# TensorE's head as loops, with the first instruction a jump to the last block of code, in a one-core decode kernel

## The chip, the cores and the metric

The kernel runs on one core of one Trainium2 chip. The metric is the device time of one execution in microseconds (us), lower is better. Before the change it was 1292.78 us (median of 3 runs, 1292.63 to 1292.84). A single profile is one execution, and its own time is quoted where that matters.

Names used below: TensorE (PE) multiplies matrices, VectorE (DVE) and ScalarE (ACT) do element-wise work, GpSimd (POOL) sets up constants, SyncE (SP) issues the large loads. A large load is spread over 16 data engines (each has 16 completions in the trace). "Products" are VectorE's multiplications of keys by the query; the first of them begins the main loop.

## The reference, cut to what matters

```python
B, Sq, D = 8, 1, 576          # A: attention over a cache
H, Sk, Dh = 32, 4096, 128     # k_cache, v_cache: (8, 32, 4096, 128) bf16, 268 MB each
F = 4608                      # B: a feed-forward layer

def reference(A_x, A_k_cache, A_v_cache, A_wq, A_wo, B_x, B_w1, B_b1, B_w2, B_b2):
    xn = layernorm(A_x)
    q = (xn @ A_wq) as heads
    p = softmax(q k^T * Dh ** -0.5)
    attention = (p v) as rows @ A_wo
    y = layernorm(xn)
    mlp = gelu(y @ B_w1 + B_b1) @ B_w2 + B_b2
    return A_x + attention + mlp
```

The two caches have to be read once: 537 MB of the 557 MB that the kernel moves.

## The kernel before

It has three stages. The **head** computes the queries, broadcasts them over the partitions, and computes the hidden layer of the feed-forward part while the first tiles of the caches arrive. The **main loop** goes through 32 pairs of a key tile and a value tile. The **tail** multiplies by `B_w2` and `A_wo`, which are loaded last.

All large loads go through SyncE's queue in order. The buffer `ring` is one block short of three tiles, and at first the head's weights lie in it too, so the loads of the main loop wait for room:

```python
    od.load("sync", "wq", ring[:, 0:WQ_END], wq_v)      # load "w q"
    od.load("sync", "w1", ring[:, W1_AT:RING], w1_v)
    load_kv(k_v, 0, 0)                                  # first key tile, "k0"
    ...
    for token in (wq_read, *head_done):                 # queries and broadcasts done
        od.wait("sync", token)
    load_kv(v_v, 0, 1)                                  # "v0", over wq
    for token in mlp_done:                              # hidden layer done
        od.wait("sync", token)
    for t in range(1, NT):
        sy.wait_ge(sem["kf"], NX * (t - 1) + 2)         # two blocks of tile t-1 multiplied
        load_kv(k_v, t, 0)                              # "k1", over w1 and the head's rooms
        sy.wait_ge(sem["vf"], t)
        load_kv(v_v, t, 1)                              # "v1"
    ...
    for n, (r0, r1) in enumerate(zip(CUTS, CUTS[1:])):  # A_wo in four pieces
        sy.dma_start(out=wo_rows(r0, r1), in_=wo_v[:, r0 * D:r1 * D]).then_inc(wo_in[-1], 16)
```

TensorE's part of the head is unrolled. The queries are 36 matmuls with 32 columns of weights each, four of which use the four column groups of the array at once (in the trace four start within 0.04 us, and the next four 0.43 us later). The broadcasts are eight times four matmuls, of which two use half the array each (two start within 0.01 us), and ScalarE copies every result out:

```python
    def queries(e):
        for c in range(WC):                             # WC = 9
            wv = wq_sb[:, c, :].rearrange("p (x m d) -> p m x d", m=M, d=Dh)
            for m in range(M):                          # M = 4, the column groups
                i = e.matmul(
                    S_ps[0][m * MP:(m + 1) * MP, :], lhsT=xT[:, c, :], rhs=wv[:, m],
                    start=(c == 0), stop=(c == WC - 1))
        return i
    ...
    for b in range(B):
        ps, key = (tot_ps, "tot") if b % 2 else (oT_ps, "oT")
        ...
        pe(["q", "sel"], [key], broadcast)              # 4 matmuls, two abreast
        act([key], [f"qb{b}"], lambda e: e.activation(out=dst, in_=t, func=ACT.Copy))
    ...
    te.br("head")                                       # TensorE's code is in blocks of its own
```

In the tail, TensorE waits for `B_w2`, then for each piece of `A_wo`. Behind the third piece are 18 matmuls, then the result is copied and stored.

The softmax here doesn't subtract the row's maximum and nothing guards it: scores larger than these inputs give would overflow.

## Time and profile before

| what | before | where it is read |
|---|---|---|
| span of the profiled run | 1291.5 us | head of the page |
| load queue's share of 16 engines' span | 99.7% | queue table |
| PE, DVE busy | 57%, 64% | table of engines |
| first product | 46.82 us | timeline of DVE |
| k1 issued | 53.53 us | timeline of SP |
| k1's data would be missed from about | 62 us | v0 has landed on its first engine at 63.49; an issue takes about 1.5 us to become data |
| third piece of A_wo landed | 1286.88 (13 engines), 1288.26 us (the last) | trace, semaphore updates of that load |

The queue table of the page comes first. Its columns are packets, MB, and the time of those packets as a share of 16 engines' span.

```profile
q1 hardware_dynamic: 10368, 556.93, 99.7%
q8 instruction: 3, 0.05, 0.0%
q10 hardware_dynamic: 38, 0.02, 0.0%
q14 instruction: 1, 0.01, 0.0%
```

The load queue leaves nothing free, so the kernel is bound by the loads, and nothing that an engine does faster can help unless it changes how the data engines are used. Four packets of *instructions* are in the table too. Their share is 0.0%, but this is the mean of 16 engines. That each of them sits on one engine, and on one that the loads use, is read from the landings below: after each of the first three, one more engine of the loads is late.

The chain of waits that ended last, in order of time (start us, us, what), ends on a load:

```profile
1259.74 28.52 DMA ring<-in_A_wo_dram
1288.26 0.04 issue
1288.31 1.29 PE acc L374 x18
1289.60 0.02 issue
1289.62 0.45 DVE fin L604
```

1288.26 is when the *last* of 16 data engines delivered its part of the third piece of A_wo; thirteen of them had delivered at 1286.88. The following table, worked out from the single packets of the trace, shows where that comes from. For a load, the spread is how much later than the first engine each of the last engines finished:

```text
kernel before        first engine, us   spread of the last three engines, us
w q                       12.6            0.50  0.51  0.75
k0                        44.2            0.51  0.75  1.75    (one engine late)
v0                        63.5            0.50  1.68  1.78    (two)
k1                        82.8            1.69  1.80  1.91    (three)
main loop from here on                    1.72  1.82  1.94    (three, to the end)

packets of instructions: queue 8 at 29.9, 76.0 and 1287.1 us (16,384 bytes, 1.02 to 1.09 us each),
                         queue 14 at 52.1 us (8,192 bytes)
```

Each fetch leaves one more engine about 1.2 us later than it was (the last values step from about 0.5 to about 1.7), and late to the end of the run: the queue is 99.7% busy.

The timeline of SP shows when loads are issued (columns: start us, us, engine line operation, out<-in):

```profile
0.00 0.38 SPq L96 DMA_DIRECT2D ring<-in_A_wq_dram  x1
...
1.26 0.33 SPq L271 DMA_DIRECT2D ring<-in_A_k_cache_dram  x1
23.95 0.33 SPq L271 DMA_DIRECT2D ring<-in_A_v_cache_dram  x1
53.53 0.33 SPq L271 DMA_DIRECT2D ring<-in_A_k_cache_dram  x1
74.24 0.33 SPq L271 DMA_DIRECT2D ring<-in_A_v_cache_dram  x1
```

Each tile takes 19.33 us of all engines. k1, issued at 53.53, had 63.49 as its deadline; v1, issued at 74.24, had 82.82.

The timelines of PE, ACT and DVE in the head (in brackets, the idle time before and what ended it):

```profile
13.84 4.01 PE L367 MATMUL s_ps<-ring 128*32 128x512 bf16 x36 [1.36 <-DVE quad L354]
18.55 0.41 PE L394 MATMUL oT_ps<-ring 128*64 128x256 bf16 x4 [0.36 <-ACT ring L385]
20.10 0.60 ACT L402 ACTIVATE qb<-oT_ps 128x512 bf16<-128x512 f32 x1
20.60 0.59 ACT L402 ACTIVATE qb<-tot_ps 128x512 bf16<-128x512 f32 x1
26.02 0.85 PE L414 MATMUL o_ps<-ring 128*32 128x384 bf16 x3 [2.80 <-DMA ring<-in_B_w_dram]
46.82 6.70 DVE L559 TENSOR_TENSOR ring<-ring,qb 128x4096 bf16<-128x4096 bf16 x3 [0.32 <-DVE hT_sb L445]
```

The queries took 4.01 us. Four broadcast matmuls took 0.41 us, less than the 0.60 us of the copy behind them, and the copies follow each other with at most 0.13 us between them: the broadcasts ran at ScalarE's pace. The layer then waited 2.80 us for `B_w1`.

### The profile page before, as it was taken

To read this page: it belongs to the slowest core of one execution; us is meant where nothing else is said; L and a number is where in the kernel's file an instruction comes from. 1 tells how busy PE (TensorE), PEld (TensorE's weight loads), DVE (VectorE), ACT (ScalarE), POOL (GpSimd) and SP (SyncE) were. 2 spreads that over 40 slices of the span, in tenths; PEclk is the share of its full clock that TensorE was granted. 3 is DMA by queue.
4 is the path that set the end of the run, shared out by engine and by line. 5 is a ranking of instruction groups with operands and counts; after the bars stand their busy time and mean duration, and the time that the engine had idled before them with its cause. 6 is when DMAs were issued, how large, how long until landed. Compare 5 with 4: busy or idle time off the path is not lost. (4 is left out here: it accounts for less than half of the span.)

```text
span 1291.5 us, 14658 instructions
## 1 busy us (share of the span) xinstructions
PE 736.8 (57%) x4707; PEld 322.3 (25%) x4707; DVE 829.4 (64%) x740; ACT 56.8 (4%) x181; POOL 2.4 (0%) x12
## 2 busy tenths in 40 slices
PE   4654565554565554665554565554566554565557
PEld 1222232222222222222222232222222222222223
DVE  2655677655677655677655677655677655577654
ACT  2000000000000000000000000000000000000000
POOL 0000000000000000000000000000000000000000
PEclk8778887778887777887777887778887777888779
DMA  9999999999999999999999999999999999999998
GB/s 419 441 427 440 430 428 449 422 428 449 422 428 449 422 430 447 422 436 440 424 436 438 426 438 434 428 442 428 428 449 422 428 449 422 428 449 422 430 447 350
DMA packets 10410, 557.02 MB, mean 431 GB/s; under 512 B 1163, under 2 KB 1188, under 8 KB 1446
## 3 DMA queue, kind: packets, MB, share of 16 engines
q1 hardware_dynamic: 10368, 556.93, 99.7%
q8 instruction: 3, 0.05, 0.0%
q10 hardware_dynamic: 38, 0.02, 0.0%
q14 instruction: 1, 0.01, 0.0%
HBM read 556.94 MB, written 0.01 MB: 431 GB/s over the span
## 5 line engine op out<-in xcount | busy, mean ns | idle before, releaser
L643 PE MATMUL s_ps<-ring,ident 128*128 x2048 | 544.5, 423 | 514.1 <-PEq L641 513.1
L559 DVE TENSOR_TENSOR ring<-ring,qb 128x4096 bf16<-128x4096 bf16 x256 | 579.2, 2283 | 281.6 <-DMA ring<-in_A_k_cache_dram 281.3
L643 PEld LDWEIGHTS s_ps<-ring,ident 128*128 128x128 bf16 x2048 | 217.4, 106 | 828.3 <-issue 678.5
L534 DVE TENSOR_REDUCE sc<-s_ps 128x32 f32<-128x512 f32 x256 | 171.8, 684 | 0.0
L662 PE MATMUL o_ps<-ring,ebd 128*32 128x512 bf16 x2048 | 116.4, 380 | 0.0
L546 DVE TENSOR_TENSOR ebd<-es,head 128x1536 bf16<-128x1536 bf16 x64 | 77.9, 1218 | 0.0
L569 DVE RECIPROCAL rec<-tot_ps 128x8 f32<-128x8 f32 x32 | 6.6, 208 | 110.7 <-PE oT_ps L670 110.7
L582 ACT ACTIVATE es<-sc 128x192 bf16<-128x192 f32 x64 | 19.8, 310 | 1104.2 <-DVE sc L534 1104.2
L662 PEld LDWEIGHTS o_ps<-ring,ebd 128*32 128x32 bf16 x2048 | 51.6, 97 | 62.5 <-issue 13.6
L670 PE MATMUL oT_ps<-selc,ob 128*128 128x8 f32 x256 | 33.9, 259 | 12.3 <-ACT ob L586 12.3
L670 PEld LDWEIGHTS oT_ps<-selc,ob 128*128 128x128 f32 x256 | 31.0, 191 | 15.2 <-ACT ob L586 15.2
L586 ACT ACTIVATE ob<-o_ps 128x512 f32<-128x512 f32 x32 | 19.1, 597 | 80.2 <-PE o_ps L662 80.2
L425 DVE TENSOR_SCALAR ring<-ring 96x384 f32<-96x384 f32 x2 | 0.7, 352 | 26.4 <-ACT ring L424 26.4
L545 DVE TENSOR_TENSOR Es<-Ep 128x1 f32<-128x1 f32 x32 | 5.1, 160 | 13.3 <-ACT es L582 13.3
L666 PEld LDWEIGHTS tot_ps<-headf,Es 128*128 128x128 f32 x64 | 9.5, 187 | 13.6 <-issue 13.6
L666 PE MATMUL tot_ps<-headf,Es 128*128 128x8 f32 x64 | 12.4, 266 | 0.0
L582 ACT ACTIVATION_READ_ACCUMULATOR es<-sc 128x1 f32 x64 | 11.9, 186 | 0.0
L414 PE MATMUL o_ps<-ring 128*32 128x384 bf16 x27 | 7.8, 860 | 2.8 <-DMA ring<-in_B_w_dram 2.8
L574 DVE TENSOR_TENSOR Ox<-on,quad 128x32 bf16 x32 | 6.2, 192 | 4.8
L414 PE MATMUL s_ps<-ring 128*32 128x384 bf16 x27 | 7.9, 862 | 0.0
L374 PE MATMUL acc<-ring,hT_sb 128*8 128x288 bf16 x72 | 6.0, 335 | 2.8 <-DMA ring<-in_B_w_dram 2.8
L336 PE MATMUL tot_ps<-ident,ring 40*128 40x16 bf16 x9 | 0.7, 204 | 11.8 <-DVE ring L314 11.8
(76 smaller groups left out, 61.2 us busy)
## 6 DMA issues: line engine op xcount, KB each, us to landing
ring<-in_B_w_dram SPq DMA_DIRECT2D x2, 5184.0 KB, 25.2
ring<-in_A_wq_dram SPq DMA_DIRECT2D x1, 4608.0 KB, 13.7
ring<-in_A_wo_dram SPq DMA_DIRECT2D x1, 1728.0 KB, 28.6
ring<-in_A_wo_dram SPq DMA_DIRECT2D x1, 1584.0 KB, 26.5
ring<-in_A_wo_dram SPq DMA_DIRECT2D x1, 1008.0 KB, 28.5
ring<-in_A_k_cache_dram SPq DMA_DIRECT2D x32, 31.9
ring<-in_A_v_cache_dram SPq DMA_DIRECT2D x32, 30.5
ring<-in_A_wo_dram SPq DMA_DIRECT2D x1, 288.0 KB, 28.8
```

The lines of the kernel that those rows point to most:

```text
L414: i = e.matmul(h_ps[j][s * MP:(s + 1) * MP], lhsT=lhsT, rhs=wv[:, r0:r0 + HK, :], **flags)
L534: ins = ve.tensor_reduce(out=sc[:, n * CB:(n + 1) * CB], in_=bank_of(x).rearrange("p (c d) -> p c d", d=DL), axis=AX.X, op=ALU.add)
L546: ve.tensor_tensor(out=ebd[:, ja:jb], in0=es[:, a:b].rearrange("p (j c) -> p j c", c=4).unsqueeze(2) .to_broadcast([P, nj, G, 4]), in1=hea ...
L559: ve.tensor_tensor(out=k, in0=k, in1=qb[:, bass.ds(t, 1), :].to_broadcast([P, CB, Dh]), op=ALU.mult,).then_inc(sem["prod"], 1)
L569: ve.reciprocal(out=rec[:], in_=tot_ps[:, :G]).then_inc(sem["rec"], 1)
L574: ve.tensor_tensor(out=Ox[:, bass.ds(t, 1)].rearrange("p o g m -> p (o g) m"), in0=on[:].unsqueeze(2).to_broadcast([P, G, M]), in1=quad[:] ...
L582: sa.activation(out=es[:, a * CB:b * CB], in_=sc[:, a * CB:b * CB], func=ACT.Exp, scale=scale, accum_out=Ep[:, i:i + 1]).then_inc(sem["x"], 1)
L586: sa.activation(out=ob[:].rearrange("r c d -> r (c d)"), in_=o_ps, func=ACT.Copy).then_inc(sem["ob"], 1)
L643: ins = te.matmul(to, lhsT=idn, rhs=k[:, :, d * DL:(d + 1) * DL], start=(d == 0), stop=(d == Dh // DL - 1))
L662: ins = te.matmul(o_ps[m * MP:(m + 1) * MP, :], lhsT=ebd[:, j].rearrange("p g c -> p (g c)"), rhs=vals[:, c:c + 4, :], start=(j < M), stop ...
L666: te.matmul(tot_ps[:, :G], lhsT=Es[:].to_broadcast([P, P]), rhs=headf[:], start=True, stop=True).then_inc(sem["vf"], 1)
L670: ins = te.matmul(oT_ps[:, :G], lhsT=ob[:, c, :], rhs=selc[:, c, :], start=(c == 0), stop=(c == 3))
```

## The change

Its intent: TensorE's program is fetched while data flows, and every fetch makes one data engine late. The author's idea was that a shorter program should need fewer fetches; that if the first instruction jumps to the last block of code, this block should be fetched before the queues are full; and that hints on the last branches should keep TensorE and VectorE from fetching beyond their ends. To shorten the program, queries and broadcasts become loops. A loop's matmul takes the places of its operands from registers. In the loops as written all of these start at partition 0, so that four matmuls abreast become four full-width ones in a row, with zeros in the weights where other column groups are. The layer goes in five groups (four of 512 columns and one of 256) in place of six of 384.

```diff
     def queries(e):
-        for c in range(WC):
-            wv = wq_sb[:, c, :].rearrange("p (x m d) -> p m x d", m=M, d=Dh)
+        def part(at, w, start):
+            wv = ring[:, bass.ds(w, HQ)].rearrange("p (x m d) -> p m x d", m=M, d=Dh)
             for m in range(M):
-                i = e.matmul(
-                    S_ps[0][m * MP:(m + 1) * MP, :], lhsT=xT[:, c, :], rhs=wv[:, m],
-                    start=(c == 0), stop=(c == WC - 1))
-        return i
+                e.matmul(
+                    S_ps[0], lhsT=xTz[:, bass.ds(at + (M - 1 - m) * MP, P)], rhs=wv[:, m],
+                    start=start and m == 0, stop=False)
+        part(0, 0, True)
+        (at, w), close = looped("queries", WC - 1, at=(M * MP, M * MP), w=(HQ, HQ))
+        part(at, w, False)
+        close()
+        return nothing(e, S_ps[0][:, :1], idn, xTz)
...
+    def broadcasts(e):
+        to = nc.alloc_registers("broadcast_to", engines=[ENG.PE])
+        nc.regs_mov(to, 0)
+        (at,), close = looped("broadcast", B, at=(0, MQ))
...
+        e.wait_ge(sem["free"], 1).then_inc(sem["free"], -1)
+        for v in range(2):
+            for k in reversed(range(NG)):
+                i = e.matmul(
+                    t[:(k + 1) * MQ, v * NH2:(v + 1) * NH2, :],
+                    lhsT=selz[:, bass.ds(at + (v * B + 1 - k) * MQ, (k + 1) * MQ)], rhs=q_v[:, k],
+                    start=True, stop=True)
+        i.then_inc(sem["full"], 1)
+        nc.regs_alu(to, NB, to, op=ALU.subtract)
+        close()
...
-    te.br("head")
+    te.br("tour")
...
+    ve.br("vector_end").branch_hint(vector_last)
+    block("vector_end", ENG.DVE)
...
+    te.br("tensor_end").branch_hint(tensor_last)
+    block("tour")
+    later(main.bb, nc.cur_bb.bb, ENG.PE)     # moves TensorE's drain and start barrier here
+    te.br("head")
+    block("tensor_end")
```

`later` moves TensorE's drain and its wait at the common start barrier behind the jump. So the other engines wait at the barrier until TensorE has jumped.

## The prediction

> **What bounds the kernel now.** DMA, end to end: the queue table gives 556.93 MB on the load queue at 99.7% of 16 engines' span; PE is busy 57%, DVE 64%. Every data engine carries 1/16 and never idles, so time lost on *one* engine is never made up: it shows where the last load waits for its slowest sixteenth. The chain of waits that ended last says this: A_wo load 28.5 us, PE acc 1.29, DVE fin 0.45, then the output store.
>
> **What the trace's packets show.** Four packets of instructions lie in the span: queue 8 (16,384 bytes, I read it as TensorE's) at 29.9, 76.0 and 1287.1 us, taking 1.02 to 1.09 us, and queue 14 (8,192 bytes; VectorE, I think) at 52.1 us. The first load's 16 completions spread over 0.75 us. After each of the first three fetches one more engine is late by about 1.2 us: the spread becomes 1.75 us by 44 us, and two, then three engines sit at +1.7 to +1.95 us from 83 us to the end. The last A_wo chunks land accordingly: 13 engines by 1287.62 us, the three late ones at 1288.77 to 1288.96; PE's last wait ends on them. [...]
>
> **The change.** Looping removes 116 TensorE instructions (791 to 675)[...]. The first jump makes TensorE fetch the last block before bulk data flows, and the hints should keep both engines from fetching past their ends. Intended: no fetch while the queues are full, so no late engine. Worth: 1288.96 - about 1287.7 = **1.2 us at the tail, all on the critical path**, if all three go. Removing only one or two gains about 0.1 us, since the remaining late engine still sets the end.
>
> **What it costs.** Queries become 36 full-width 512-column matmuls in sequence instead of four abreast: 4.0 us now; then about 9 cold at 0.427 us and 27 warm at 0.22 = about 10 us (estimate). Broadcasts stay bound by eight 0.6 us ACT copies. The layer begins when the copies end (about 30.5) instead of on w1 (26.0); five groups instead of six, the same columns, about 13 us as before; GELU chain about 6.5. Tile 0 starts at about 51 instead of 46.8. Slack: the second k load was issued at 53.5 with data queued to 63.5; the second v load at 74.2 with data to 82.8. Four microseconds later still leaves about 2 us after issue latency: no bubble, cost 0. TensorE reaching the start barrier a few us late delays only the k load (24 us of data queued ahead) and set-up work with slack.
>
> **Predicted:** 1291.7 us, 8 in 10 within 1291.1 to 1292.9. Faster by over 2%: 0.5%; within 2%: 98.5%; slower: 1%.
>
> **Right if:** queue 8 and VectorE's queue have no packets between about 5 us and the tail; the 16 completions of mid-run loads stay within about 0.8 us; the last A_wo landing is about 1.2 us earlier; first DVE product at 49 to 53 us; DMA share unchanged or nearer 100% with no gap at 60 to 90 us.
>
> **Wrong if:** the jump's fetch itself falls into the first data packets and leaves one engine 1.2 us late (no gain); a next-block fetch still comes when TensorE reaches its last block near 1280 us; VectorE's fetch stays; or the looped queries or broadcasts stall (branches, semaphores) over 6 us longer than now, and the second v load is issued after 81 us, when DMA runs dry and the kernel is 1 to 3 us slower.

The forecast's sum: 1292.8 us before, less 1.2 at the tail, plus nothing for the head, is about 1291.6, put at 1291.7. That 116 fewer instructions, with the jump and the hints, would take away all the fetches after the start was the author's estimate. In the estimate of the queries, 0.427 us is the spacing of the nine steps of the queries in the trace of the kernel before, and 0.22 that of its 512-column matmuls near 70 us; that nine would be slow was an estimate too (13 were).

## The result, and the profile after

The kernel after the change took 1296.62 us (median of 6 runs, 1296.29 to 1297.52), the kernel before 1292.94 us (6 runs of the same rounds). The ratio is 1.003, with a 95% interval from 1.0017 to 1.0043: slower by 0.3%, 3.7 us, which is inside the class "within 2%". A ratio here and below is the mean time of one kernel's fast runs over that of the other's of the same rounds, so it is not quite the ratio of the medians quoted. The six times lie in two groups, 1296.3 to 1296.8 and 1297.4 to 1297.5; the profiled run (1297.42 us, span 1296.1) is of the second.

The queue table after the change:

```profile
q1 hardware_dynamic: 10368, 556.93, 99.4%
q8 instruction: 1, 0.02, 0.0%
```

The fetches are gone, as intended: one is left, at 4.68 us, and queue 14 has none in the span. But the share of the load queue *fell*, from 99.7 to 99.4% of a longer span. The bytes are the same in both, so about 0.3% of the span, some 4 us, is time in which the queue had nothing to do. The windows of 4 us find it. Before (columns: window, its length, then busy time of PE, PEld, DVE, ACT, POOL with instructions in brackets, granted PE clock, DMA share, GB/s):

```profile
60.00:64.00 4.00, 3.10 (x15) 1.17 (x12) 4.00 (x3) 0.00 (x0) 0.00 (x0) 1.00 1.21 524
64.00:68.00 4.00, 2.02 (x9) 0.78 (x8) 4.00 (x4) 0.46 (x2) 0.00 (x0) 1.00 0.68 295
68.00:72.00 4.00, 3.57 (x42) 1.65 (x46) 3.58 (x6) 0.35 (x2) 0.00 (x0) 1.00 1.13 492
```

and after:

```profile
60.00:64.00 4.00, 1.61 (x4) 0.66 (x5) 4.00 (x2) 0.00 (x0) 0.00 (x0) 0.50 0.64 279
64.00:68.00 4.00, 4.00 (x15) 1.64 (x14) 4.00 (x4) 0.00 (x0) 0.00 (x0) 0.76 0.72 246
68.00:72.00 4.00, 3.38 (x15) 1.27 (x13) 4.00 (x3) 0.00 (x0) 0.00 (x0) 1.00 0.64 279
```

A single window swings, because a packet counts where it ends, but over the three the mean is 437 GB/s before and 268 after: data for 4.6 us at 437 GB/s is missing. The cause is in the timeline of SP:

```profile
7.22 0.33 SPq L292 DMA_DIRECT2D ring<-in_A_k_cache_dram  x1
39.45 0.33 SPq L292 DMA_DIRECT2D ring<-in_A_v_cache_dram  x1
66.35 0.33 SPq L292 DMA_DIRECT2D ring<-in_A_k_cache_dram  x1
87.21 0.33 SPq L292 DMA_DIRECT2D ring<-in_A_v_cache_dram  x1
```

k1 was issued at 66.35 us where the queue ran empty at 63.43; v1 was issued at 87.21, when the first engine was finishing k1 (87.24) and had nothing behind it. (A tile takes 19.33 us, so k1's data flowed in full from 87.24 - 19.33 = 67.9 us: an issue takes about 1.5 us to become data.) The tiles' first landings, 19.33 us apart when the queue is full, were 63.43, 87.24 and 108.08, so the dry stretches of the first engine are 23.81 - 19.33 = 4.5 us and 20.84 - 19.33 = 1.5 us. From v1 on the first engine lands 5.93 us later than in the kernel before, and 5.83 us later at the last tile of the caches: the main loop itself is unchanged.

The issue is late because the head is. The timelines of POOL, PE, ACT and DVE that answer to those shown of before:

```profile
7.21 0.20 POOL L299 MEMSET ident<- 128x128 bf16 x1 [6.78 <-POOLq L785]
15.78 10.79 PE L411 MATMUL s_ps<-ring 128*128 128x512 bf16 x36 [0.47 <-DVE ring L364]
27.81 0.95 PE L449 MATMUL b_ps<-ring 128*128 128x256 bf16 x4 [0.89 <-PEq L446]
29.16 0.95 PE L449 MATMUL b_ps<-ring 128*128 128x256 bf16 x4 [0.40 <-PEq L446]
...
31.79 6.86 PE L449 MATMUL b_ps<-ring 128*128 128x256 bf16 x20 [0.38 <-PEq L446]
34.60 0.60 ACT L462 ACTIVATE qb<-b_ps 128x512 bf16<-128x512 f32 x1 [0.76 <-PE b_ps L449]
35.96 0.60 ACT L462 ACTIVATE qb<-b_ps 128x512 bf16<-128x512 f32 x1 [0.76 <-PE b_ps L449]
39.43 1.08 PE L475 MATMUL o_ps<-ring 128*32 128x512 bf16 x4 [0.78 <-ACT qb L462]
59.80 6.70 DVE L619 TENSOR_TENSOR ring<-ring,qb 128x4096 bf16<-128x4096 bf16 x3 [0.31 <-DVE hT_sb L505]
```

The first product came 12.98 us later. Along the head, from these lines:

| step | before | after | later by |
|---|---|---|---|
| start of the queries (barrier passed at 7.15 instead of 1.19 us) | 13.84 | 15.78 | 1.9 |
| the queries | 4.01 | 10.79 | 6.8 |
| end of the queries to the first broadcast | 0.70 | 1.24 | 0.5 |
| first broadcast to the last copy's end (after: to the layer's start) | 5.3 | 11.6 | 6.3 |
| last copy to the layer's start (before: a wait for B_w1) | 2.2 | (in the line above) | -2.2 |
| the layer and GELU to the first product | 20.8 | 20.4 | -0.4 |

ScalarE tells that the broadcasts changed their limit: before each copy but the first it now waits 0.71 to 1.20 us for PE, where it had waited 0.13 us at most. One iteration takes 1.31 to 1.36 us, in two ways. In each of the first three, PE needs 0.95 us for four 256-column matmuls in a row (pairs abreast took 0.41) and then waits 0.36 to 0.40 us for its sequencer, which does the branch, the semaphores and the register arithmetic (in TensorE's raw record 0.21 to 0.23 us for the loop's branch and 0.03 to 0.08 us for each register operation). In the last five PE does not pause: 20 matmuls take 6.86 us, or 1.36 us for four, while the granted clock was 0.50 (windows of 33 to 38 us). That clock is not what makes the broadcasts long: the iterations ahead of it are as long, and in the kernel before, where the clock fell to 0.52 as well (21 to 24 us), four matmuls took 0.64 us.

The jump at the start took 6.48 us in TensorE's record, while the second, back to the head, took 0.19 us. POOL's 6.78 us of idle time is the other engines' view of it.

At the other end, the landing of the third A_wo piece:

```text
third piece of A_wo, landing by engine, us     first    13th      14th     15th     16th
before                                        1286.38  1286.88   1288.06  1288.15  1288.26
after                                         1292.20  1292.58   1292.60  1292.63  1292.78
```

At this end no engine is late any more, as the change intended (the section on e4 shows that the dry stretch did this, and not the missing fetches alone). The first engine lands 1292.20 - 1286.38 = 5.82 us later, the last is 1.30 us nearer to the first (0.58 us behind it in place of 1.88), and 4.52 us are left, which is the difference of the last landing, 1292.78 - 1288.26. The profiled runs differ by 1297.42 - 1292.88 = 4.54 us.

The chain of waits does not say this. Its last lines after the change are

```profile
1257.43 24.97 DMA ring<-in_B_w_dram
1282.40 0.04 issue
...
1287.47 6.64 PE acc L423 x100
1294.12 0.02 issue
```

It ends on PE now, since PE reached its last 18 matmuls just as the third piece landed, and it reaches back only to a load that was on time in its queue. A hole in the queue at 64 us is no wait of anything in the chain, and only the landings and the windows show it.

### The profile page after: what moved, and what is told of

Read it like the earlier page. It is cut to its first block, busy times and chain, and to the rows that moved or that the text cites. A ratio compares the mean times of both kernels' runs of the same rounds, so it can differ in the third digit from the quotient of the medians.

```text
span 1296.1 us, 14773 instructions
## 1 busy us (share of the span) xinstructions
PE 741.2 (57%) x4698; PEld 324.9 (25%) x4698; DVE 829.5 (64%) x740; ACT 57.0 (4%) x181; POOL 3.4 (0%) x13
## 3 DMA queue, kind: packets, MB, share of 16 engines
q1 hardware_dynamic: 10368, 556.93, 99.4%
## 5 line engine op out<-in xcount | busy, mean ns | idle before, releaser
L705 PE MATMUL s_ps<-ring,ident 128*128 x2048 | 535.0, 416 | 514.9 <-PEq L703 514.8
L705 PEld LDWEIGHTS s_ps<-ring,ident 128*128 128x128 bf16 x2048 | 214.7, 105 | 822.4 <-issue 669.8
L629 DVE RECIPROCAL rec<-b_ps 128x8 f32<-128x8 f32 x32 | 6.7, 208 | 110.7 <-PE b_ps L732 110.7
L732 PE MATMUL b_ps<-selc,ob 128*128 128x8 f32 x256 | 33.9, 259 | 12.3 <-ACT ob L646 12.3
L732 PEld LDWEIGHTS b_ps<-selc,ob 128*128 128x128 f32 x256 | 31.0, 191 | 15.2 <-ACT ob L646 15.2
L475 PE MATMUL o_ps<-ring 128*32 128x512 bf16 (+1 forms) x40 | 12.8, 1079 | 0.8 <-ACT qb L462 0.8
L728 PEld LDWEIGHTS b_ps<-headf,Es 128*128 128x128 f32 x64 | 9.5, 187 | 13.6 <-issue 13.6
L728 PE MATMUL b_ps<-headf,Es 128*128 128x8 f32 x64 | 12.4, 266 | 0.0
L411 PE MATMUL s_ps<-ring 128*128 (+1 forms) x36 | 10.8, 474 | 0.5 <-DVE ring L364 0.5
L449 PE MATMUL b_ps<-ring 128*128 128x256 bf16 (+1 forms) x32 | 9.7, 364 | 2.0 <-PEq L446 2.0
## 6 DMA issues: line engine op xcount, KB each, us to landing
ring<-in_A_v_cache_dram SPq DMA_DIRECT2D x32, 30.5
```

The costliest lines, as they stand in the source:

```text
L411: e.matmul(S_ps[0], lhsT=xTz[:, bass.ds(at + (M - 1 - m) * MP, P)], rhs=wv[:, m], start=start and m == 0, stop=False)
L475: i = e.matmul(h_ps[j][s * MP:(s + 1) * MP], lhsT=lhsT, rhs=wv[:, r0:r1, :], **flags)
L705: ins = te.matmul(to, lhsT=idn, rhs=k[:, :, d * DL:(d + 1) * DL], start=(d == 0), stop=(d == Dh // DL - 1))
L728: te.matmul(tot_ps[:, :G], lhsT=Es[:].to_broadcast([P, P]), rhs=headf[:], start=True, stop=True).then_inc(sem["vf"], 1)
L732: ins = te.matmul(oT_ps[:, :G], lhsT=ob[:, c, :], rhs=selc[:, c, :], start=(c == 0), stop=(c == 3))
```

## The experiments

The theory after the result: **lateness**. The head passed the point (about 62 us for k1's issue, about 55 us for the first product) from which the queue runs dry; the dry time is lost and the late engines' 1.2 us are gained. Rivals: the start jump delays everything; the looped code slows the main loop; the fetches of instructions cost more or less than the 1.2 us read off the landings.

| run | median (range), us | ratio to before (95%) | first product, us | k1 issued |
|---|---|---|---|---|
| before (profile) | 1292.94 (1292.63 to 1293.21) | | 46.82 | 53.53 |
| after | 1296.62 (1296.29 to 1297.52) | 1.003 (1.0017 to 1.0043) | 59.80 | 66.35 |
| e1, after, no jump | 1295.7 (1295.28 to 1297.27) | 1.0024 (1.0007 to 1.004) | 57.72 | 64.24 |
| e11, after, barrier before the jump | 1296.06 (1295.08 to 1297.11) | 1.0027 (1.001 to 1.0044) | 57.67 | 63.83 |
| e2, after, old queries | 1293.26 (1292.96 to 1294.91) | 1.0006 (0.9989 to 1.0022) | 52.92 | 59.64 |
| e3, after, old broadcasts | 1293.08 (1293.05 to 1293.14) | 1.0001 (0.9984 to 1.0018) | 50.39 | 56.90 |
| e4, e1 and e2 together | 1292.9 (1292.78 to 1293.0) | 0.9999 (0.9982 to 1.0016) | 51.28 | 58.11 |
| e8, as e4, no "tour" block | 1293.02 (1292.87 to 1293.51) | 1.0001 (0.9984 to 1.0017) | 51.37 | |
| e5, before, first product 12.7 us later | 1297.97 (1297.41 to 1298.19) | 1.0038 (1.0021 to 1.0055) | 59.56 | 65.91 |
| e12, before, 8.3 us later | 1293.79 (1293.52 to 1293.9) | 1.0007 (0.9991 to 1.0024) | 55.12 | 61.82 |
| e6, before, 4 us later | 1292.91 (1292.74 to 1293.28) | 1.0 (0.9984 to 1.0017) | 50.83 | 57.28 |
| e7, before, VectorE's hint | 1293.01 (1292.7 to 1293.22) | 1.0 (0.9984 to 1.0017) | 46.91 | 53.62 |
| e9, before, 8 useless one-row loads | 1297.25 (1297.08 to 1297.29) | 1.0034 (1.0017 to 1.0051) | 50.97 | |
| e10, before, one load of 8 rows | 1295.17 (1294.91 to 1295.7) | 1.002 (1.0003 to 1.0036) | | |
| e13, before, which engines (one look) | 1293.27 | | | |
| e14, e7, which engines (one look) | 1293.3 | | | |
| e15, e7, third piece in other shares | 1297.59 (1295.78 to 1298.56) | 1.0038 (1.0024 to 1.0052) | 46.74 | 53.01 |
| e16, before, the same shares | 1297.12 (1296.76 to 1297.59) | 1.0032 (1.0016 to 1.0047) | 46.62 | 52.90 |
| e17, e10's rows four partitions apart | 1293.47 (1293.28 to 1293.73) | 1.0002 (0.9986 to 1.0019) | 47.38 | 53.60 |
| e18, third piece split by columns | 1293.18 (1292.84 to 1293.35) | 1.0001 (0.9984 to 1.0018) | | |

The times of before in the rounds of each run had medians from 1292.85 to 1293.0.

### Lateness alone: e5, e6, e12

These are the kernel before with a useless reduction on VectorE just ahead of the main loop. Nothing of the change is in them. Each of `n` output columns costs about 4.3 us; e6 has n = 1, e12 n = 2, e5 n = 3.

```diff
     te.br("head")
+    ve.tensor_reduce(
+        out=sc[:, :n], in_=qb[:].rearrange("p n d -> p (n d)").unsqueeze(1)
+        .to_broadcast([P, n, NT * Dh]), axis=AX.X, op=ALU.add)
```

> Kernel before, with one useless VectorE reduction of about 13 us put before its first tile; TensorE's code is untouched. Theory (lateness alone makes the loss): first DVE product near 59.7, second k load near 66.3, second v load near 87: the queue runs dry twice for 5.9 us in all; late engines that were made late before the dry stretch catch up in it. 1296.5 to 1299. Rival (the loss comes from the new TensorE code or the fetch): no change, 1292.9.

> The same with a reduction of about 4.3 us: what I had predicted for the change. Theory: inside the slack of about 6 us, so no dry stretch and no cost: 1292.9 within 0.3. Rival (every us of lateness costs): 1297.

> Kernel before with a useless VectorE reduction of about 8.7 us before the first tile. Theory (cost only beyond the slack, which the load issues set): first DVE product near 55.5, second k load near 62.2, second v load near 83.0; data of the loads ahead ends at 63.5 and 82.8 on the earliest engine, and an issue takes about 1.5 us to become data, so the first dry stretch is about 0.3 us and the second about 1.7 us, part of it taken by the engines that were late anyway: 1293.0 to 1294.6. Rival (cost grows in proportion, 5.1 us for 13): 1296.3.

The timelines of DVE and SP in e5:

```profile
46.69 12.95 DVE L590 TENSOR_REDUCE sc<-qb 128x3 f32<-128x12288 bf16 x1
59.56 6.68 DVE L559 TENSOR_TENSOR ring<-ring,qb 128x4096 bf16<-128x4096 bf16 x3
...
65.91 0.33 SPq L271 DMA_DIRECT2D ring<-in_A_k_cache_dram  x1
86.97 0.33 SPq L271 DMA_DIRECT2D ring<-in_A_v_cache_dram  x1
```

The queue was dry for 3.75 and 1.86 us, 5.6 in all, and the kernel took 5.0 us longer than before. The late engines caught up in the dry stretches here too: the spread of a load's engines fell from 1.52 us (v0) to 0.48 us (v1). So lateness by itself makes the whole loss of the change and a little more; what was left of the gain from the fetches cannot be seen beside it. e5's result is in its expected range. e5's profiled run and that of the change are 1297.86 and 1297.42 us; the medians are 1.35 us apart because most runs of the change are in its lower group of times.

e6 with 4 us costs nothing and e12 with 8.3 us costs 0.9 us (both as expected), with dry stretches of 0.28 and 1.02 us. The free slack of the head thus ends between a first product at 51 and one at 55 us.

### Undoing the loops one at a time: e2 and e3

e2 puts the old unrolled queries back into the kernel after the change, e3 the old broadcasts.

```diff
     def queries(e):                                  # e2
-        ... (the loop of the change)
+        for c in range(WC):
+            ... (the four matmuls abreast of the kernel before)
```

```diff
-    pe(["q", "sel"], ["oT", "tot"], broadcasts)      # e3
-    ... (the loop, and ScalarE's waits on "full")
+    for b in range(B):
+        ... (the kernel before's broadcasts and copies)
```

> Changed kernel with the old queries, four abreast and unrolled. Theory: queries take 4.0 us instead of 10.8, first DVE product near 53.0, second k load near 59.6, second v load near 80.4, both before the queue runs dry: no dry stretch, 5.9 us regained; but the engine made late by the start fetch is then never caught up with, so the last A_wo landing is one late engine (about 1.2 us) over the rest: 1292.4 to 1293.0. Rival A (jump and fetch): 1296.6. Rival C (steady state slower in the changed kernel): more than 1295.

> Changed kernel with the old eight broadcasts, unrolled, instead of the loop. Theory: broadcasts take 5.3 us instead of 11.5, first DVE product near 53, no dry stretch or one under 0.5 us: 1292.4 to 1293.2, as with the old queries. Rival (queries alone are to blame): 1296.

In e2 the queries took 4.03 us again and the first product moved to 52.92; in e3 it moved to 50.39:

```profile
50.39 6.70 DVE L606 TENSOR_TENSOR ring<-ring,qb 128x4096 bf16<-128x4096 bf16 x3 [0.31 <-DVE hT_sb L492]
```

Each of the two gives back nearly the whole 3.7 us (to 1293.26 and 1293.08). (e3 is in its expected range, e2 0.26 us above it.) Their effects do not add: 59.8 is about 5 us beyond the free slack, and either of them takes away 7 to 9 us. It follows that neither loop alone is "the" cause. The prediction's allowance of about 6 us for the queries would have fitted into the slack; with the broadcasts' 6 us, which it had put at nothing, it did not.

Neither run gained anything over the kernel before, though both lie before the dry point. Both programs are longer than 677 instructions (e2 has about 722), and the fetches came back: queue 8 at 4.57, 37.37 and 1281.66 us in e2, at 4.58, 35.08 and 1281.91 us in e3. Late engines are back with them.

### The jump: e1, e11, e4 and e8

e1 leaves TensorE's barrier where it was, ahead of the jump:

```diff
     block("tour")
-    later(main.bb, nc.cur_bb.bb, ENG.PE)
     te.br("head")
```

> Changed kernel, but TensorE passes the start barrier first and jumps afterwards. Theory (the head is late, so two loads are issued after the queue has run dry): barrier back at 1.2 us instead of 7.1; the jump still takes about 6.5 us, but ends before TensorE's first matmul is due at 11.8; queries start at 13.8 instead of 15.8, first DVE product near 57.8 instead of 59.8, second k load issued near 64.4; the first dry stretch shrinks by 2 us, the second stays: about 1294.7 us (before + 1.8). Rival A (the jump and its fetch themselves cost the time, head lateness is harmless): time unchanged at 1296.6. Rival B (barrier delay of 6 us is the whole loss): back to about 1292.9 or below.

This did not test quite what it was made for. With nothing left in the block, the toolchain removed the jump altogether: the trace has no jump and no fetch at the start, but one at 63.75 us. The first product came at 57.72, and the time was 1295.7 us with 2.28 + 1.56 us dry: still most of the loss, with no jump at all (1 us above the expected 1294.7). e11 keeps the jump, after the barrier, by putting a wait that is long satisfied into the block:

```diff
     block("tour")
-    later(main.bb, nc.cur_bb.bb, ENG.PE)
+    te.wait_ge(od.sem("gpsimd"), 1)
     te.br("head")
```

> Changed kernel; TensorE passes the start barrier, then jumps to a block in its last line of code that holds one more wait (so that the toolchain cannot fold the jump away), then goes to the head. Theory: packet on queue 8 near 5 to 6 us, jump about 6.5 us long, over by 8 us, before the first matmul at 11.8; first DVE product near 57.7, both dry stretches left: 1294.5 to 1295.7, as in the run where the jump was folded away. If the jump had a cost other than the barrier's delay, it is slower than that run by over 1 us.

The jump again took 6.5 us, from 1.47 to 7.99 us, but only TensorE waited. The first product was at 57.67, the time 1296.06, 0.4 us above the expected range. So the delay of the other engines at the barrier is worth about 2 us of lateness. What it is worth in time is not settled: the medians of e11 and the change differ by 0.6 us, but the times of both scatter over more than 1 us, and their profiled spans differ by 2.1 us (1294.0 against 1296.1), as do their dry stretches (3.7 us in e11, 5.9 in the change). Most of the loss is there without that delay, so it is the smaller part.

e4 (no jump, old queries) and e8 (the same with the "tour" block taken out and the branch to it undone) come before the dry point:

> Both of the above: first DVE product near 51. Theory: no dry stretch, one late engine: 1292.4 to 1293.0, the same as with the queries alone, because slack that is not needed gains nothing. If the barrier costs time by itself, this one is faster than queries alone by 1 us or more.

> Changed kernel with old queries, both prefetch hints, but no jump: is the hint alone enough to fetch TensorE's last block at the start? If yes: one packet on queue 8 near 5 us, none later, barrier at 1.2 us, one late engine, 1292.4 to 1293.0. If not: a packet on queue 8 later, near 30 to 90 us, when TensorE first enters its second block, again one late engine, the same time. Either way no dry stretch.

Both took the time of the kernel before, 1292.9 and 1293.02 us. e8 also answers its question: the hint alone did not fetch the last block at the start, since queue 8 has its first packet at 37.16 us and another at 1281.77. In e4 exactly one engine is late, by 1.93 us, from the fetch at 37.27 us until another fetch at 1281.6 makes a second one late, and the last landing of A_wo is at 1288.96, the very time of the kernel before with its three late engines. One late engine is as bad as three. This is what the prediction had said ("the remaining late engine still sets the end"). It also suggests, though no run with the change's short program and a head on time was made, that the change would have gained nothing had its head been on time: the single fetch at 4.68 us that the jump causes made one engine late as well. After the first load one engine was 1.73 us behind the first one (0.75 us in the kernel before), and it stayed so (1.82 us at v0) until the dry stretch let it catch up (0.63 us at k1, 0.58 us afterwards). The "regained" 1.3 us in the change's result come from the hole in the queue, not from the absence of fetches alone. e11 shows the same: an engine 1.35 us late until the dry stretch, and none afterwards.

### VectorE's fetch: e7

```diff
+    vector_last = nc.mark_branch_hint_location(ENG.DVE)
...
+    ve.br("vector_end").branch_hint(vector_last)
+    block("vector_end", ENG.DVE)
```

> Kernel before, plus only the prefetch hint for VectorE's last jump and its end block. If queue 14's packet at 52 us is VectorE's, it goes, and one of the three late engines with it; two (from queue 8 at 30 and 76 us) stay late by 1.2 us, so the time changes by 0.0 to 0.15 us only: 1292.8. If the late engines' count did not matter but their sum did: 0.4 us gained.

The packet of queue 14 at 52 us was gone, two engines were late instead of three, and the time did not change. This part of the change works and is worth nothing while another engine is late.

### Extra bytes on known engines: e9, e10 and e17

These add 0.11 MB to the kernel before, eight useless rows of 13,536 bytes, in the head. Over 16 engines that would be 0.25 us (one data engine moves 65,536 bytes in 2.42 us, 27.1 GB/s, in the trace of the kernel before).

```diff
+    extra = [od.load("sync", f"extra{i}", ring[i:i + 1, XA:TILE], k_v[i:i + 1, :TILE - XA])
+             for i in range(8)]                                                        # e9
+    extra = [od.load("sync", "extra", ring[:8, XA:TILE], k_v[:8, :TILE - XA])]         # e10
+    extra = [od.load("sync", "extra", ring[0:32:4, XA:TILE], k_v[:8, :TILE - XA])]     # e17
```

> Kernel before with eight useless loads of one row of 13.5 KB each, queued between the w1 and the first k load. A test of the step that one data engine's lost time is never made up: if such loads fall on one and the same engine (0.5 us each at 27 GB/s), that engine is late by 4 us to the end of the run, and the time grows by 2.2 to 4 us although only 0.25 us worth of bytes were added over 16 engines. If each falls on another engine, the time grows by 0.0 to 0.5 us. The 16 completion times of the following loads tell which.

> The same bytes as one load of eight rows, which should fall on eight engines, 0.5 us each: eight engines half a microsecond later; time grows by 0.5 us at most, if one of the three late engines is among the eight, or not at all.

> e10 with one thing changed: its load of eight useless rows goes to partitions 0, 4, 8 ... 28 instead of 0 to 7; same bytes, same source, same eight engines. Theory [...]0.5 us, so 1293.3 to 1293.6 and no long packets. Rival (the small load itself or its source rows, which the k load reads too, cost 2.3 us): 1295.2 again.

In e9 all eight loads ran on the same engine, one after another, five of them in 0.51 to 0.52 us and three in 0.94 to 1.01. e10's one load of eight rows has eight landings, and e13's loads of 2 to 16 rows have as many as rows; a single row went to one engine here. The last piece of A_wo landed by 1289.32 us on 15 engines and at 1293.40 on one. The chain of waits followed that one engine:

```profile
1264.22 28.46 DMA ring<-in_A_wo_dram
1292.68 0.04 issue
1292.72 1.29 PE acc L378 x18
```

The eight packets took 5.5 us of that engine from 25.18 us on. The last landing of k0 was 4.5 us later than in the kernel before (50.83 against 46.35), and that of the third piece of A_wo, over 1240 us later, 4.4 us (1292.68 against 1288.26), which is the 4.4 us by which the time grew, a little over the expected 2.2 to 4. So here a single late engine set the end.

e10 was a miss. The same rows in one load went to eight engines and should have cost them 0.5 us each, yet the time rose by 2.3 us. e17 changes only the destination partitions and costs 0.5 us. e10's eight rows go to partitions 0 to 7, e17's to every fourth one from 0 to 28. In the traces the eight packets took 0.51 to 1.58 us in e10 and 0.51 us each in e17, and 19 of the key and value packets in the first 90 us took over 2.6 us in e10 where 3 did in e17 and in the kernel before. So the place of the rows is the cause: eight neighbouring partitions slow the small load and the large loads around it, eight that lie four apart do not. By what mechanism is not shown; the expectation of e17, 0.5 us, is one row's packet (0.51 us measured).

### Which engines are late: e13 and e14

e13 adds sixteen tiny loads of 1 to 16 rows behind the last piece of A_wo. A load of n rows has n completions in the trace. The author assumed that each load takes the engines of the one before it and one new engine, called n-1 here; then the time of the new one's first completion says whether it is late. e14 is the same on top of e7.

```diff
+    for n, p in enumerate(probes, 1):
+        sy.dma_start(out=small[:n, (n - 1) * 32:n * 32],
+                     in_=k_v[:n, (n - 1) * 32:n * 32]).then_inc(p, 16)
```

> Kernel before with sixteen tiny useless loads of 1 to 16 rows (64 bytes each) after the last A_wo load. If a load of n rows falls on the first n engines, then the number of its completions that are late by over 0.9 us, as n grows, steps up by one at each late engine's number: three steps in all, always in place if the engine of an instruction fetch is fixed. Time about 1293 to 1294.

> The same with VectorE's hint: two steps instead of three, two of the same places.

```text
first completion of the engine that joins, us
             engine 3     engine 12    engine 13    all others
e13          1288.75      1289.15      1289.16      1287.4 to 1288.3
e14 (hint)   1287.89      1289.20      1289.15      1287.3 to 1288.3
```

Engine 3 is made late by VectorE's fetch (queue 14), since it is punctual with the hint (1287.89 us in place of 1288.75), and engines 12 and 13, late in both runs, by TensorE's two (queue 8 at 29.9 and 76.0 us). The numbers rest on the assumption: the traces show how many engines a load took, and not which. Both runs, and e15, e16 and e18, also have a packet of 8,192 bytes on queue 14 near 1265 us, with VectorE's hint too. Whose it is was not tested.

### Taking bytes off the late engines: e15, e16 and e18

With these numbers, e15 (with VectorE's hint) and e16 (without) split the third piece of A_wo in loads of 80, 24 and 24 partitions, meant to give the late engines fewer of its rows. Which engines such loads take was assumed and is not shown by a trace, so the shares worked out from it are cut from the expectations; the landing at about 1287.4 us expected of e15 rested on them.

```diff
+    SHARES = {n: [(0, P)] for n in range(len(CUTS) - 1)}
+    SHARES[2] = [(0, 80), (80, 104), (104, P)]
-        sy.dma_start(out=wo_rows(r0, r1), in_=wo_v[:, r0 * D:r1 * D]).then_inc(wo_in[-1], 16)
+        for a, z in SHARES[n]:
+            sy.dma_start(
+                out=wo_rows(r0, r1)[a:z], in_=wo_v[a:z, r0 * D:r1 * D]).then_inc(wo_in[-1], 16)
-        te.wait_ge(wo_in[n], 16)
+        te.wait_ge(wo_in[n], 16 * len(SHARES[n]))
```

> The kernel before with VectorE's hint (two late engines, 12 and 13) and the third piece of A_wo split in three loads[...]. Theory (the late engines' 1.2 us sets the end): the third piece lands at about 1287.4 instead of 1288.26, and the time is 1292.0 to 1292.3, 0.7 to 0.9 us less than before. Rival (their lateness doesn't set the end, or the bytes spread otherwise): 1292.9 or more.

> The same split without the hint: engine 3, which VectorE's fetch makes late, stays late[...], so no gain and perhaps a loss: 1293.0 to 1293.4, with one engine's landing of the third piece at 1288.3 to 1288.6. Rival (which engine is late is not settled by the byte counting): equal to e15.

Both lost over 4 us: a clear miss. The median packet of 8,064 bytes in the third piece took 0.59 us, where it had taken 0.305, and from 1284 to 1288 us (packets counted where they end) the queue moved 230 GB/s where it had moved 339. The timeline of PE in e15 now has two waits for A_wo:

```profile
1287.96 1.51 PE L376 MATMUL acc<-ring,OT 128*8 128x288 bf16 x22 [1.92 <-DMA ring<-in_A_wo_dram]
1291.20 1.27 PE L376 MATMUL acc<-ring,OT 128*8 128x288 bf16 x18 [1.72 <-DMA ring<-in_A_wo_dram]
```

e18 splits the same piece in three loads too, but by columns, so that each has all 128 partitions:

```diff
+    third = (CUTS[3] - CUTS[2]) * D // 3
+    SHARES = {2: [(i * third, (i + 1) * third) for i in range(3)]}
...
+                out=wo_rows(r0, r1)[:, a:z], in_=wo_v[:, r0 * D + a:r0 * D + z]).then_inc(wo_in[-1], 16)
```

> The kernel before with the third piece of A_wo in three loads as e15, but split by columns: each of the three has all 128 partitions[...]. Theory[...]: no loss, 1292.8 to 1293.3, packets at the usual pace. Rival (more and smaller loads at the end cost the 4 us by themselves): 1296 or more.

It took 1293.18 us, 0.2 us from the kernel before. So more and smaller loads were not the cause, nor the extra fetch near 1265 us, which e18 has as well. What is left is how the loads of e15 and e16 lie over the partitions (80, 24 and 24 of them in place of all 128); in e10 and e17 the partitions alone made a difference (2.3 against 0.5 us). The mechanism is not shown, and neither is whether an engine's lateness can be moved to another in some other way.

A second flaw of e15 lies in its expectation: even with a punctual third piece PE would have gained at most 0.9 us, its wait before the last 18 matmuls in the kernel before, and where PE is slower in the tail nothing. In e18's profile the 36 matmuls behind B_w2 took 4.48 us, in that of before 3.67, and PE did not wait for A_wo at all.

No run beat the kernel before. The best of those made from the change, e4, equals it.

## Why the prediction was wrong

It said 1291.7 us, 1291.1 to 1292.9; the median was 1296.62. The class, within 2%, came true; the direction and the range did not.

1. **"Broadcasts stay bound by eight 0.6 us ACT copies." This is the step that failed, together with the next.** The copies were the limit only while four matmuls took 0.41 us two abreast. In the loop they are full-width and in a row, 0.95 us at the full clock with 0.4 us of branch, semaphore and register work on top, or 1.36 us at half the clock: 1.31 to 1.36 us an iteration against 0.60, 6.3 us over the head. The layer began at 39.43 us where about 30.5 was predicted, 8.9 us later: 6.3 of them are the broadcasts', 1.9 the barrier's (the next step), and 0.8 the queries'. The full-width cost was applied to the queries and forgotten for the broadcasts, though both have the same cause.
2. **"TensorE reaching the start barrier a few us late delays only the k load and set-up work with slack."** The barrier was passed 6 us late, and the queries began 1.9 us later. This is the smaller part: in e11, where only TensorE waits, most of the loss stays (1296.06 us).
3. **"The queries ... about 10 us" was right** in its sum (10.79; the first 13 matmuls were 0.43 us apart and the others 0.22, where the estimate had 9 and 27), and so was the layer (13.9 us before, about the same after).
4. **"Tile 0 starts at about 51 ... no bubble, cost 0."** It started at 59.80. The mechanism was in the text as a way to be wrong ("if the looped queries or broadcasts stall over 6 us longer than now ... 1 to 3 us slower"), with a deadline for the second v load of 81 us that the trace confirms; that load came at 87.21. The size was too small: 5.9 us of dry queue, 4.5 of them ahead of the k load and not of the v load. e5, e6 and e12 show that this alone gives the loss.
5. **"Worth 1.2 us, if all three go."** The fetches after 5 us went, all of them. The landing of the last sixteenth moved 1.3 us nearer to the first, as said. But "the jump's fetch itself falls into the first data packets and leaves one engine 1.2 us late" is what happened too, and the late engine caught up only because the queue ran dry. e4 and e8, where one late engine of another fetch costs as much as three, suggest that without the dry stretch the gain would have been about nothing, so that the prediction's best case was out of reach with this design, even with a fast head. This is argued and not shown: no run has the change's short program with a head on time, and none has punctual engines without a dry stretch.
6. **"Removing only one or two gains about 0.1 us" was right**: e7 (two late engines) and e4 (one) are within 0.1 us of before (three).
7. The count was off without consequence: the "791 instructions" include labels, the trace's programs have 783 and 677. At a length of 677 there was no fetch after 4.68 us; at about 722 (e2) there was one at 1281.66 us.

What stays open: why the change, e1 and e11 have two groups of times about 1 us or more apart, and e2 one time of four 1.5 us above the others (each kernel has one profile, so this cannot be told); whether a queue without any late engine and without a dry stretch would be 1.2 us faster; and whether a fetch at the start can be had before any data flows, which no kernel here managed.

## What to carry to other kernels

When a kernel is bound by full load queues, ask of every change to a stage off the critical path by how many microseconds it may slip before the next load's issue misses its deadline, and add up *all* its slips, each priced with the width and order of the new instructions: here 7 us of the 13 fitted, and the rest left the queue dry almost one for one (5.9 us, of which 1.3 were lateness that the engines would have had anyway). Time taken from a single data engine shows at the end once that engine is the last, however small its share of the bytes (e9: 4.4 us), and removing some of several such things gains nothing while another stays (e4, e7). Small loads should spread over the partitions: eight rows on neighbouring partitions cost 2.3 us, four apart 0.5 us (e10, e17).
